# A transformer block with linear attention: attention outputs and down projections as pairs of 64-row matmuls in two parts

## The chip, the core and the metric

The kernel runs on one core of a Trainium2 chip. Its engines are TensorE (PE, with its weight loads shown as PEld), VectorE (DVE), ScalarE (ACT), GpSimd (POOL) and SyncE (SP), which issues nearly all DMAs. The metric is the device time of one execution in microseconds (us); the median of several runs counts.

## The reference

One layer over 2048 tokens of 448 features, all in bf16. A is linear attention with 16 heads of 28 features, B a gated MLP with 1792 hidden features.

```python
phi = lambda t: jnp.where(t > 0, t + 1, jnp.exp(t)) + 1e-6
def A(x, wqkv, wo):                      # x is the layer-normed input
    q, k, v = split_heads(x @ wqkv)      # 16 heads of 28
    pq, pk = phi(q), phi(k)
    kv = einsum("bhsd,bhse->bhde", pk, v)
    z = einsum("bhsd->bhd", pk)
    o = einsum("bhqd,bhde->bhqe", pq, kv) / (einsum("bhqd,bhd->bhq", pq, z)[..., None] + 1e-6)
    return join_heads(o) @ wo
def B(x, w_gate, w_up, w_down):
    return (gelu_tanh(x @ w_gate) * (x @ w_up)) @ w_down
h = x + A(layernorm(x), wqkv, wo)
out = h + B(layernorm(h), w_gate, w_up, w_down)
```

## The kernel before

The 2048 tokens are 16 tiles of 128. Every operation is a task in a graph (`G.add`); the graph finds what each task waits for by the buffers that it reads and writes. The order of the tasks on each engine is written out by hand as five lists of task numbers (`ORDERS`, lines 15 to 51): PE, ACT, DVE, POOL, SP. Each engine takes its list strictly in order, and waits on counters of the other engines; TensorE never waits for itself.

First stage (to about 39 us). Each tile is layer-normed (L348 and L349 for mean and variance), transposed (by TensorE for the first four tiles, by DMA on SP for the others, L390) and projected to q and k (L404, four matmuls of 128 rows and 448 columns a tile). ScalarE makes exp and relu of q into `eq` and `pq` (L431, L432). phi(k) is multiplied with the normed input into four PSUM banks (L423), and line 462 makes of it the 16 matrices kv. Line 466 masks them to blocks of four heads (`kvm`), and line 471 multiplies each block with its rows of wo: `w2`, four groups of 112 rows. So the attention output is, tile by tile, (pq / den) @ w2.

`a2_pair(p)` handles two tiles, one after the other on VectorE. L483 and L484 finish phi(q); L488 (GpSimd, once VectorE) multiplies it with z; L491, L493 and L494 make 1/den; L495 writes pq/den into `pqn`, with each group of 112 features padded to 128. A DMA transpose on SP (L510; for the first pair TensorE, L504) makes `pqnT` of it. Line 523 is the attention output: for each tile four matmuls of 112 rows and 448 columns that add up in one PSUM bank. L529 adds the residual, then come layer norm and the transpose `hnT` (L558, L560, L561; seven 128-feature slices, so that every 64-feature segment lies in both halves of the partitions).

`gu_chunk` makes gate and up (in chunks of 2, 2, 4, 4 and 4 tiles): line 603 takes rows 0 to 63 for the gate, line 605 rows 64 to 127 for up, as two 64-row matmuls at once, seven pairs for each 128 hidden features. A task gu has 512 columns of gate in one bank and 512 of up in another; two such pairs of banks alternate (`BK_G`, `BK_U`). ScalarE makes the gelu (L623), VectorE the product `hh` (L625), which frees the bank.

`b2_tile(t)` is the down projection of one tile: 14 matmuls of 128 rows and 448 columns (L575), the residual (L579) and the output DMA (L580). The last tile goes in two halves of 224 columns. The down weights `wd_sb` are loaded by one DMA of 1568 KB, which the list of SP has behind the transposes of tiles 2 and 3.

On TensorE's list the work of later tiles stands between that of earlier ones: attention outputs of the pairs 2 to 7 and down projections stand in eight blocks between gate-and-up tasks.

Of the kernel before, what the change touches and what calls it, by code (L numbers as in the profile page):

```python
# [5 lines left out]
BF16 = mybir.dt.bfloat16  # L6
# [44 lines left out]
)  # L51


class _Buf:
    __slots__ = ("name", "writer", "readers")

    def __init__(self, name):
        self.name = name
        self.writer = None
        self.readers = []  # L60

# [5 lines left out]
class _Graph:  # L67
# [7 lines left out]
    def add(self, eng, fn, r=(), w=(), name="", kind="op", after=(), mw=False, cost=()):  # L75
# [6 lines left out]
        def dep(d, k):  # L82
            if d is None or d is t:
                return
            if d.eng == eng == "pe":
                t.after.append(d)
                return
# [83 lines left out]
def bass_sequential_preLN__linear_attn_block__glu_gated_geglu__prompt_kernel(  # L171
# [5 lines left out]
    NK = 7  # L177
# [513 lines left out]
```

## Time and profile before

| | |
|---|---|
| median of 3 runs | 193.96 us (193.29 to 194.66) |
| span of the profiled execution, first to last instruction | 192.2 us (the page gives no other time of it) |
| TensorE busy | 187.5 us, 98%, 1572 matmuls |
| VectorE busy | 131.7 us, 69% |
| ScalarE, GpSimd busy | 78.1 us, 50.6 us |
| gate and up (L603, L605), in the chain that ended last | 34% and 5% (they run side by side) |
| down projections (L575), in that chain | 22% |
| attention outputs (L523), in that chain | 5% |

The chain that ended last is followed back from the last instruction: at each step to what released it, or to the instruction before it on its engine. A row of a group has line, engine, operation, output and inputs, shape and count, then the busy time in us, the mean of one in ns, and the idle time of the engine before it. Durations of matmuls overlap: what one costs is the distance from its start to the next one's. "64*128" is the height of the array in use and its columns, "64x512" rows and columns of the moving operand.

### The profile page before, as it was taken

The numbers are of one execution on the slowest core, as the hardware profiler recorded it, in microseconds if no ns is written. First come the engines' busy times: TensorE is split into PE (matmuls) and PEld (weight loads), VectorE is DVE, ScalarE is ACT, GpSimd is POOL, SyncE is SP. The second block draws the span as 40 slices with busy tenths as digits, with TensorE's granted clock in tenths as the row PEclk, the third lists the DMA queues.
The fourth block names the chain that finished last, engine by engine and source line by source line (L and its number), as shares of the span: only waits on it lengthen the run. The fifth ranks groups of instructions, "written<-read, shape, count | busy, mean of one in ns | idle before, by whom it ended". The sixth has DMA issues, their size and how long they took to land.

```text
span 192.2 us, 4152 instructions
## 1 busy us (share of the span) xinstructions
PE 187.5 (98%) x1572; PEld 108.7 (57%) x1572; DVE 131.7 (69%) x355; ACT 78.1 (41%) x226; POOL 50.6 (26%) x92
## 2 busy tenths in 40 slices
PE   7989999999999999999999999999999999999994
PEld 7544554554778777564444655545556655445454
DVE  2899988999999998979957446736544542244412
ACT  3697836599954243044044420024444420044200
POOL 7068520560263287404190000450000000000000
PEclk9999999999999999999999999999999999999999
DMA  6966558998205866520042124305600001010011
GB/s 192 372 186 82 109 104 172 224 217 122 58 0 112 201 206 124 123 54 1 4 78 46 38 49 95 95 1 124 143 0 3 0 3 46 3 48 3 0 48 48
DMA packets 35331, 16.97 MB, mean 88 GB/s; under 512 B 27696, under 2 KB 34032, under 8 KB 35312
## 3 DMA queue, kind: packets, MB, share of 16 engines
q1 hardware_dynamic: 35168, 16.60, 38.4%
q8 instruction: 12, 0.20, 0.4%
q10 hardware_dynamic: 144, 0.11, 0.2%
q14 instruction: 7, 0.06, 0.1%
HBM read 8.26 MB, written 1.84 MB: 53 GB/s over the span
## 4 chain that ended last, share of the span: by engine, by line
PE 84%; DMA 6%; DVE 4%; ACT 3%; POOL 1%; issue 0%; SPq 0%; DVEq 0%; POOLq 0%
PE ps L603 34%; PE ps L575 22%; PE ps L404 10%; PE ps L423 6%; PE ps L523 5%; PE ps L605 5%; DMA wd_sb<-in_B_w_down_dram 4%; DMA x_sb<-in_A_x_dram 2%; DVE hh L625 1%; DVE st L348 1%; ACT eq L431 1%; ACT pq L432 1%; DVE x_sb L529 1%; PE ps L471 0%; ACT e L415 0%
## 5 line engine op out<-in xcount | busy, mean ns | idle before, releaser
L605 PE MATMUL ps<-hnT,wgu_sb 64*128 64x512 bf16 (+1 forms) x490 | 86.6, 334 | 0.0
L603 PE MATMUL ps<-hnT,wgu_sb 64*128 64x512 bf16 (+1 forms) x490 | 86.4, 333 | 0.1
L623 ACT ACTIVATE gl<-ps 128x256 bf16<-128x256 f32 x112 | 37.1, 380 | 83.7 <-PE ps L605 81.8
L625 DVE TENSOR_TENSOR hh<-ps,gl 128x256 bf16<-128x256 f32 x112 | 42.9, 418 | 30.9 <-ACT gl L623 30.7
L603 PEld LDWEIGHTS ps<-hnT,wgu_sb 64*128 64x128 bf16 x490 | 45.3, 94 | 28.0 <-issue 2.6
L605 PEld LDWEIGHTS ps<-hnT,wgu_sb 64*128 64x128 bf16 x490 | 42.7, 94 | 4.8 <-DVE hh L625 2.0
L575 PE MATMUL ps<-wd_sb,hh 128*128 128x448 bf16 (+1 forms) x238 | 43.6, 342 | 0.1
L575 PEld LDWEIGHTS ps<-wd_sb,hh 128*128 128x128 bf16 x238 | 23.0, 98 | 20.1 <-issue 0.8
L404 PE MATMUL ps<-wqk_sb,xnT 128*128 128x448 bf16 x128 | 27.6, 352 | 0.5 <-ACT xnT L383 0.5
L488 POOL TENSOR_TENSOR t<-pq,zbc 128x448 f32<-128x448 bf16 x15 | 16.6, 1117 | 39.0 <-DVE pq L484 22.2
L579 DVE TENSOR_TENSOR x_sb<-ps,x_sb 128x448 bf16<-128x448 f32 (+1 forms) x17 | 10.0, 591 | 18.2 <-PE ps L575 18.2
L348 DVE BATCH_NORM_STATS2 st<-x_sb 128x6 f32<-128x448 bf16 x32 | 19.3, 612 | 3.7 <-DMA x_sb<-in_A_x_dram 3.7
L404 PEld LDWEIGHTS ps<-wqk_sb,xnT 128*128 128x128 bf16 x128 | 12.1, 98 | 11.6 <-ACT xnT L383 0.8
L423 PE MATMUL ps<-pk,xnn 128*128 128x448 bf16 x64 | 14.1, 352 | 0.0
L523 PE MATMUL ps<-w,pqnT 112*128 112x448 bf16 x64 | 13.6, 353 | 0.3 <-DVE mv L349 0.3
L529 DVE TENSOR_TENSOR x_sb<-ps,x_sb 128x448 bf16<-128x448 f32 x16 | 9.7, 613 | 2.7 <-PE ps L523 2.7
L558 POOL TENSOR_SCALAR hn<-x_sb,nm,rs 128x448 bf16<-128x448 bf16 x14 | 10.5, 755 | 0.8 <-POOL rs L361 0.2
L415 ACT ACTIVATE e<-ps 128x448 bf16<-128x448 f32 x16 | 8.5, 540 | 5.3 <-PE ps L404 5.2
L352 POOL TENSOR_SCALAR nm<-mv 128x1 f32<-128x1 f32 (+1 forms) x19 | 4.1, 220 | 25.1 <-DVE mv L349 24.5
L495 DVE TENSOR_TENSOR pqn<-pq,rd 128x448 bf16<-128x448 bf16 x16 | 9.9, 641 | 0.0
L417 DVE SCALAR_TENSOR_TENSOR pk<-ps,e 128x448 bf16<-128x448 f32 x16 | 9.8, 615 | 0.2
L523 PEld LDWEIGHTS ps<-w,pqnT 112*128 112x128 bf16 x64 | 5.6, 97 | 7.2 <-issue 1.3
(65 smaller groups left out, 130.1 us busy)
## 6 DMA issues: line engine op xcount, KB each, us to landing
out_dram<-x_sb SPq DMA_DIRECT2D x15, 112.0 KB, 1.8
wd_sb<-in_B_w_down_dram SPq DMA_DIRECT2D x1, 1568.0 KB, 7.1
x_sb<-in_A_x_dram SPq DMA_DIRECT2D x3, 448.0 KB, 5.7
wgu_sb<-in_B_w_gate_dram SPq DMA_DIRECT2D x1, 896.0 KB, 12.3
wgu_sb<-in_B_w_up_dram SPq DMA_DIRECT2D x1, 896.0 KB, 16.4
wqk_sb<-in_A_wqkv_dram SPq DMA_DIRECT2D x1, 672.0 KB, 5.0
wgu_sb<-in_B_w_gate_dram SPq DMA_DIRECT2D x1, 672.0 KB, 6.1
wgu_sb<-in_B_w_up_dram SPq DMA_DIRECT2D x1, 672.0 KB, 8.6
```

Of the source, the lines that this page charges most:

```text
L348: op("dve", lambda e: e.bn_stats(st[:, t, :], src_ap), [b_src], [b_st[t]], "bnst%s_%d" % (tag, t))
L404: ins = e.matmul(ps[:, bk, 0:D], xnT[:, t, k, :], wqk_sb[:, k, c0:c0 + D], start=(k == 0), stop=(k == 3))
L423: ins = e.matmul(ps[:, BK_PT[c], 0:D], xnn[:, t % XN_R, c * 128:(c + 1) * 128], pk[:, ip, :], start=(t == 0), stop=(t == T - 1))
L488: op(eng, lambda e, t=t, n=n: e.tensor_tensor(t1[:, n, :], pq[:, t, :], zbc[:, :], ALU.mult), [b_pq[t]] + b_z, [b_t1[n]], "t1%s_%d" % (eng ...
L523: ins = e.matmul(ps[:, BK_OUT[n], 0:D], pqnT[0:GW, i2, n, g, :], w2[:, g, :], start=(g == 0), stop=(g == NG - 1))
L529: op("dve", lambda e, t=t, bo=bo: e.tensor_tensor(x_sb[:, t, :], ps[:, bo, 0:D], x_sb[:, t, :], ALU.add), [b_ps[bo], b_x[t]], [b_x[t]], "h ...
L558: op("pool", lambda e, t=t, sh=sh: e.tensor_scalar(hn[:, sh, 0:D], x_sb[:, t, :], nm2[:, t:t + 1], rs2[:, t:t + 1], ALU.add, ALU.mult), [b ...
L575: ins = e.matmul(psO, hh[:, j, (t % HR) * 128:(t % HR + 1) * 128], wd_sb[:, j, c0:c1], start=(j == 0), stop=(j == NJ - 1))
L603: e.matmul(psG[:, jj * N:(jj + 1) * N], wgu_sb[A_, k, j * 128:(j + 1) * 128], hnT[A_, ka_, c0:c0 + N], start=(k == 0), stop=(k == NK - 1))
L605: ins = e.matmul(psU[:, jj * N:(jj + 1) * N], wgu_sb[B_, k, j * 128:(j + 1) * 128], hnT[B_, kb_, c0:c0 + N], start=(k == 0), stop=(k == NK ...
L623: G.add("act", lambda e, gi=gi, cs_=cs_, psG=psG: e.activation(gl[:, gi, cs_], psG[:, cs_], AF.Gelu_apprx_tanh), r=[b_ps[BK_G[i]]], w=[b_g ...
L625: op("dve", lambda e, dst=dst, srcU=srcU, srcL=srcL: e.tensor_tensor(dst, srcU, srcL, ALU.mult), [b_ps[BK_U[i]], b_glh], [b_ar[j_][t % HR] ...
```

## The change

1. Attention output, pairs 1 to 7. `pqn` holds the 448 features of two tiles one after the other without padding, so that the transpose gives seven slices of 128 for both tiles. Each tile's seven 64-feature segments lie alternately in the lower and the upper half of the partitions, the second tile's the other way round. A pair of 64-row matmuls takes one segment of each tile at once, into the two tiles' banks. Part A has four such pairs, part B (the halves exchanged) three. The first pair of tiles keeps four full-height matmuls a tile.
2. `w2` is made in four slices of 128 rows instead of four of 112 (7 matmuls instead of 4, from `kvz`, which lies in `hh` and is zeroed by GpSimd early; a small VectorE copy makes its last slice). Two DMAs of 168 KB make `w2s`, the same slices with the halves exchanged, in the space of `pt_sb`.
3. Down projection, tiles 0 to 13. `b2_pair` takes two tiles: part A multiplies rows 0 to 63 of one tile beside rows 64 to 127 of the other, for all 14 groups of hidden features, part B the halves exchanged, into the same two banks. The last two tiles keep the old form.
4. Part B waits until part A has ended (`sync`): TensorE waits on its own counter.
5. VectorE's attention steps of the pairs 2 to 7 take both tiles in one instruction, and ScalarE's L493 too; GpSimd's product with z stays tile by tile.
6. The five lists are new. On TensorE's, with gu2 and gu4 the gate-and-up tasks:

```
... q_13 q_15 q_12 q_14 trh_0 trh_1 outA_1 outB_1 gu2_0 gu2_1 outA_2 gu2_2 gu2_3 outB_2
gu2_4 gu2_5 outA_3 gu2_6 outB_3 downA_0 gu2_7 downB_0 gu2_8 ... gu2_11 outA_4 gu2_12 outB_4
gu2_13 downA_1 gu4_14 gu4_15 outA_5 gu4_16 outB_5 gu4_17 downB_1 outA_6 gu4_18 ... gu4_22
outB_6 gu4_23 ... gu4_27 downA_2 gu4_28 outA_7 gu4_29 outB_7 gu4_30 ... gu4_33 downB_2
gu4_34 downA_3 gu4_35 ... gu4_40 downB_3 gu4_41 ... gu4_45 downA_4 gu4_46 ... gu4_49 downB_4
gu4_51 gu4_50 downA_5 gu4_53 gu4_52 downB_5 gu4_55 gu4_54 downA_6 down224_15 downB_6
down448_14 down224_15
```

On SP's: `oT_1 dws0 dws1 oT_2 dwd oT_3 hT_2 hT_3 oT_4 ...` (oT: transposes of `pqn`, dws: the copies of `w2`, dwd: the down weights, hT: transposes of `hn`); before, `oT_1 oT_2 oT_3 hT_2 hT_3 dwd oT_4 ...`. On GpSimd's, `ones mones eps mhalf wqkpad ones2 kvzpad ptpad ident ...`; before, `eps ones wqkpad ident wvpad ones2 ...`.

The core of the diff:

```diff
-    def add(self, eng, fn, r=(), w=(), name="", kind="op", after=(), mw=False, cost=()):
+    def add(self, eng, fn, r=(), w=(), name="", kind="op", after=(), mw=False, cost=(), sync=()):
...
+        self.dep(t, sync)
...
-        kvm = sb("kvm", [GW, NG, GW], BF16)
-        w2 = sb("w2", [GW, NG, D], BF16)
+        w2 = sb("w2", [128, 4, D], BF16)
...
-        pqn = sb("pqn", [128, 2, 2, NG, 128], BF16)
-        pqnT = sb("pqnT", [128, 2, 2, NG, 128], BF16)
+        pqn = sb("pqn", [128, 2, 1024], BF16)
+        pqnT = sb("pqnT", [128, 2, 8, 128], BF16)
...
+        kvz = hh[0:GW, 6:9, :].rearrange("p a b -> p (a b)")
+        w2s = pt_sb[:, 0:3, :]
...
+        op("pool", lambda e: e.memset(kvz[:, GW:15 * GW], 0.0), [], [b_kvm], "kvzpad")
...
+        for c in range(4):
+            def fw2(e, c=c):
+                gs = (c, c + 1) if c < 3 else (3,)
+                ins = None
+                for g in gs:
+                    ins = e.matmul(ps[:, BK_W2[c], 0:D], kvc(g, c), wo_sb[:, g, :], start=(g == gs[0]), stop=(g == gs[-1]))
+                return ins
...
+        for h, (to, of) in enumerate(((A_, B_), (B_, A_))):
+            dma("sp", w2s[to, :, :], w2[of, 0:3, :], [b_w2s[h]], "dws%d" % h, r=b_w2[0:3], after=xts[-1:])
...
+                i, b2 = 2 * (p % 2), slice(a, a + 2)
+                op("dve", lambda e: e.tensor_scalar(eq[:, b2, :], eq[:, b2, :], 1.0, EPS, ALU.min, ALU.add), b_eq[b2], b_eq[b2], "cqP_%d" % p)
+                op("dve", lambda e: e.tensor_tensor(pq[:, b2, :], pq[:, b2, :], eq[:, b2, :], ALU.add), b_eq[b2] + b_pq[b2], b_pq[b2], "aqP_%d" % p)
...
+                op("dve", lambda e: e.tensor_tensor(
+                    pqn[:, i2, 0:2 * D].rearrange("p (h d) -> p h d", d=DH), pq[:, b2, :].rearrange("p n (h d) -> p (n h) d", d=DH),
+                    rd[:, i:i + 2, :].rearrange("p n h -> p (n h)").unsqueeze(2).to_broadcast([128, 2 * H, DH]), ALU.mult),
+                   b_pq[b2] + b_rd[i:i + 2], b_pqn[i2], "pnP_%d" % p)
...
-                            ins = e.matmul(ps[:, BK_OUT[n], 0:D], pqnT[0:GW, i2, n, g, :], w2[:, g, :], start=(g == 0), stop=(g == NG - 1))
...
+                for part, segs in (("A", (0, 2, 4, 6)), ("B", (1, 3, 5))):
+                    def foutp(e, segs=segs):
+                        ins = None
+                        for sg in segs:
+                            ra, rb = (A_, B_) if sg % 2 == 0 else (B_, A_)
+                            e.matmul(ps[:, BK_OUT[0], 0:D], pqnT[ra, i2, sg // 2, :], w2[ra, sg // 2, :], start=(sg == 0), stop=(sg == 5))
+                            ins = e.matmul(ps[:, BK_OUT[1], 0:D], pqnT[rb, i2, 3 + (sg + 1) // 2, :], (w2 if sg == 6 else w2s)[rb, sg // 2, :], start=(sg == 0), stop=(sg == 5))
+                        return ins
+                    parts.append(G.add("pe", foutp, r=b_pqnT[i2] + b_w2 + b_w2s, w=[b_ps[b_] for b_ in BK_OUT], name="out%s_%d" % (part, p), sync=parts[-1:]))
...
+        def b2_pair(p):
+            a = 2 * p
+            sl = [slice((t % HR) * 128, (t % HR + 1) * 128) for t in (a, a + 1)]
+            parts = []
+            for half in range(2):
+                def fdp(e, W, half=half):
+                    ins = None
+                    for j in range(NJ):
+                        W(j)
+                        for n in range(2):
+                            rows = (A_, B_)[(n + half) % 2]
+                            ins = e.matmul(ps[:, BK_O[n], 0:D], hh[rows, j, sl[n]], wd_sb[rows, j, :], start=(half == 0 and j == 0), stop=(half == 1 and j == NJ - 1))
+                    return ins
+                parts.append(G.add("pe", fdp, r=[(b_ar[j][t % HR], j if j >= NJ - 2 else 0) for j in range(NJ) for t in (a, a + 1)] + [b_wd],
+                                   w=[b_ps[b_] for b_ in BK_O], name="down%s_%d" % ("AB"[half], p), mw=True, sync=parts[-1:]))
```

More of the change, by code (lines that the diff above doesn't have):

```diff
@@ L73, in __init__, with dep @@
         self.order = None
-    def add(self, eng, fn, r=(), w=(), name="", kind="op", after=(), mw=False, cost=()):
+    def dep(self, t, ds):
+        for d in ds:
+            if d not in t.deps:
+                t.deps.append(d)
+                d.ncons += 1
+                t.dep_at[d.idx] = 0
+    def add(self, eng, fn, r=(), w=(), name="", kind="op", after=(), mw=False, cost=(), sync=()):
         t = _Task()
@@ L85, in dep @@
             if d.eng == eng == "pe":
+                if d in t.deps:
+                    return
                 t.after.append(d)
@@ L470, in bass_sequential_preLN__linear_attn_block__glu_gated_geglu__prompt_kernel @@
-        for g in range(NG):
-            G.add("pe", lambda e, g=g: e.matmul(ps[0:GW, BK_W2[g], 0:D], kvm[:, g, :], wo_sb[:, g, :], start=True, stop=True),
-                  r=[b_kvm, b_wo], w=[b_ps[BK_W2[g]]], name="w2_%d" % g)
-            if g % 2 == 0:
-                op("act", lambda e, g=g: e.activation(w2[:, g, :], ps[0:GW, BK_W2[g], 0:D], AF.Identity), [b_ps[BK_W2[g]]], [b_w2[g]], "evwA_%d" % g)
-            else:
-                op("dve", lambda e, g=g: e.tensor_copy(w2[:, g, :], ps[0:GW, BK_W2[g], 0:D]), [b_ps[BK_W2[g]]], [b_w2[g]], "evwD_%d" % g)
+           [b_ps[BK_KV], b_mask, b_kvm], [b_kvm], "kvm")
@@ new lines, in bass_sequential_preLN__linear_attn_block__glu_gated_geglu__prompt_kernel, with kvc @@
+        b_kvd = _Buf("kvd")
+        op("dve", lambda e: e.tensor_copy(kvz[:, 4 * D:4 * D + 64], kvz[:, 4 * D - 64:4 * D]), [b_kvm], [b_kvd], "kvd")
+        def kvc(g, c):
+            o = g * D + c * 128 if c < 3 else 4 * D - 64
+            return kvz[:, o:o + 128]
+        for c in range(4):
[5 more added lines that the diff above has]
+                return ins
+            G.add("pe", fw2, r=[b_kvm, b_wo] + ([b_kvd] if c == 3 else []), w=[b_ps[BK_W2[c]]], name="w2_%d" % c)
+            if c % 2 == 0:
+                op("act", lambda e, c=c: e.activation(w2[:, c, :], ps[:, BK_W2[c], 0:D], AF.Identity), [b_ps[BK_W2[c]]], [b_w2[c]], "evwA_%d" % c)
+            else:
+                op("dve", lambda e, c=c: e.tensor_copy(w2[:, c, :], ps[:, BK_W2[c], 0:D]), [b_ps[BK_W2[c]]], [b_w2[c]], "evwD_%d" % c)
@@ L489, in a2_pair @@
[L489 to L498 removed]
+            pst = D if p else 512
@@ L515, in a2_pair, with fout @@
                 dma("sp", wd_sb[:, :, :], B_w_down.rearrange("(j p) n -> p j n", p=128), [b_wd], "dwd", after=[G.all[-1]])
-            for ns in ((0,), (1,)) if p == 0 else ((0, 1),):
-                def fout(e, W, i2=i2, ns=ns):
-                    ins = None
-                    for m, n in enumerate(ns):
+            if p == 0:
+                for n in range(2):
+                    def fout(e, W, n=n):
+                        ins = None
                         for g in range(NG):
-                            W(4 * m + g)
-                            ins = e.matmul(ps[:, BK_OUT[n], 0:D], pqnT[0:GW, i2, n, g, :], w2[:, g, :], start=(g == 0), stop=(g == NG - 1))
-                    return ins
-                G.add("pe", fout, r=[(b_pqnT[i2][n], 4 * m) for m, n in enumerate(ns)] + [(b_w2[g], g) for g in range(NG)],
-                      w=[(b_ps[BK_OUT[n]], 4 * m) for m, n in enumerate(ns)], name="out%d_%d" % (len(ns), a + ns[0]), mw=True)
+                            W(g)
+                            ins = e.matmul(ps[:, BK_OUT[n], 0:D], pqnT[:, i2, 4 * n + g, :], w2[:, g, :], start=(g == 0), stop=(g == NG - 1))
+                        return ins
+                    G.add("pe", fout, r=[(b_pqnT[i2][n], 0)] + [(b_w2[g], g) for g in range(NG)], w=[(b_ps[BK_OUT[n]], 0)], name="out1_%d" % (a + n), mw=True)
+            else:
+                parts = []
[8 more added lines that the diff above has]
+                    parts.append(G.add("pe", foutp, r=b_pqnT[i2] + b_w2 + b_w2s, w=[b_ps[b_] for b_ in BK_OUT], name="out%s_%d" % (part, p), sync=parts[-1:]))
             for t in (a, a + 1):
@@ L635, in bass_sequential_preLN__linear_attn_block__glu_gated_geglu__prompt_kernel @@
             gu_chunk(t0, nt)
-            for t in range(t0, t0 + nt):
-                b2_tile(t)
+            for t in range(t0, t0 + nt, 2):
+                if t < T - 2:
+                    b2_pair(t // 2)
+                else:
+                    b2_tile(t)
+                    b2_tile(t + 1)
             t0 += nt
```

67 lines of the change are left out of this document (40 added, 27 removed), and 68 rows, old and new, of the table ORDERS.

## The prediction

> **What bounds the kernel now.** I read the page's first lines, then the chain of waits, then the stretches, and last TensorE's own timeline around the places that the change touches.
>
> ```profile
> PE 187.5 (98%) x1572; PEld 108.7 (57%) x1572; DVE 131.7 (69%) x355; ACT 78.1 (41%) x226; POOL 50.6 (26%) x92
> PEclk9999999999999999999999999999999999999999
> PE 84%; DMA 6%; DVE 4%; ACT 3%; POOL 1%; issue 0%; SPq 0%; DVEq 0%; POOLq 0%
> ```
>
> TensorE (PE) works almost without a hole at full clock and carries 84% of the chain. So the question is what its stream costs: how many matmuls, at what distance, and what holes. The stretches say where holes could come from.
>
> ```profile
> 50.00:60.00 10.00, 10.00 (x153) 7.53 (x150) 9.55 (x28) 6.52 (x15) 4.92 (x7) 1.00 0.28 54
> 130.00:140.00 10.00, 10.00 (x96) 5.32 (x94) 5.42 (x18) 4.40 (x14) 0.00 (x0) 1.00 0.58 126
> ```
>
> From 10 to 80 us VectorE (third pair of numbers) is busy 9 to 10 of every 10 us, later about half. A late VectorE step can stop TensorE only in the first part.
>
> The distance of matmuls is read from their starts, since the durations (353 and 377 ns) overlap.
>
> ```profile
> 111.53 0.38 PE L603 MATMUL ps<-hnT,wgu_sb 64*128 64x512 bf16 x1
> 111.59 0.38 PE L605 MATMUL ps<-hnT,wgu_sb 64*128 64x512 bf16 x1
> 111.90 1.69 PE L523 MATMUL ps<-w,pqnT 112*128 112x448 bf16 x8
> 113.42 1.30 PE L575 MATMUL ps<-wd_sb,hh 128*128 128x448 bf16 x6
> ```
> ```profile
> 93.69 1.49 PE L575 MATMUL ps<-wd_sb,hh 128*128 128x448 bf16 x7
> 95.11 0.39 PE L603 MATMUL ps<-hnT,wgu_sb 64*128 64x512 bf16 x1
> 95.11 0.39 PE L605 MATMUL ps<-hnT,wgu_sb 64*128 64x512 bf16 x1
> 95.34 0.38 PE L603 MATMUL ps<-hnT,wgu_sb 64*128 64x512 bf16 x1
> ```
> ```profile
> 88.26 1.62 PE ps L523 x8
> 89.88 5.30 PE ps L575 x28
> 118.89 1.52 PE ps L523 x8
> 120.40 5.30 PE ps L575 x28
> ```
>
> Three things are to be seen. First, 28 full-height matmuls of 448 columns take 5.30 us, 189 ns each, or 0.422 ns a column; the pairs L603/L605 of 64 rows run side by side, both in one slot of 215.5 ns for 512 columns (0.421 a column). Second, after a pair the same eight matmuls of L523 cost 1.62 us, after a full-height matmul 1.52. Third, the last L575 before 95.11 starts at 93.69 + 6 x 0.189 = 94.82, so the first pair comes 0.285 later instead of 0.189. Each change between full height and 64-row pairs costs about 0.095 us, in either direction (308 ns instead of 215 at 111.90, 201 instead of 108 in the two-tile chunks). There are 16 such changes: eight blocks of L523/L575 stand between the gate-and-up pairs.
>
> The other holes behind 11 us are few: 0.18 at 18.54 (a transpose's landing), 0.12 at 39.93, 0.10 at 44.31, 0.42 at 47.77, 0.24 at 65.41, 0.20 at 70.30.
>
> ```profile
> 47.77 1.67 PE L523 MATMUL ps<-w,pqnT 112*128 112x448 bf16 x8 [0.26 <-DVE mv L349]
> PEld ps L575 <- DMA wd_sb<-in_B_w_down_dram: 0.4, 1, 0.4
> wgu_sb<-in_B_w_up_dram SPq DMA_DIRECT2D x1, 896.0 KB, 16.4
> DMA to landing us min/median/max: 3.0/3.1/4.1
> ```
>
> The first is a timeline row, then one of the waits, one of the page's DMA issues, and one of line L510's own view. The hole at 47.77 is really the first transposed load of L510, issued at 43.55 and landing 4.1 later, at 47.6, behind the up weights (issued at 30.4, landed at 46.8). The one at 65.41 is tile 3's transpose (issued at 61.1, landed at 65.3), the one at 70.30 the down weights.
>
> **The change, part by part.** The sum is made against the profiled span, 192.2; the page has no other time of that execution. The median of the runs, 193.96, lies 1.76 above it, which I carry as a constant.
>
> *Attention output.* Seven pairs of tiles need 7 slots each (448 features in seven 64-row segments) instead of 8 (four 112-row groups a tile): -7 x 0.189 = -1.32 us. All of it was on TensorE's path. The W2 products go from 4 matmuls to 7, ahead of the pairs in the same stream: +3 x 0.189 = +0.57.
>
> *Down projections.* 14 tiles go from 14 matmuls each to 28 half-height matmuls for two tiles in each of two parts: 28 slots for two tiles, as before. At the pairs' rate 448 columns take 188.6 ns against 189.3: 196 x 0.7 = -0.13. The width of 448 for a pair is not in the trace; its bounds are the 256 pairs (107.7 ns, 0.421 a column) and the 512 pairs (0.421), so I take no more uncertainty than +-0.2 us there.
>
> *Changes of shape.* Of 16, 4 remain: the transposes ahead of the first out pair, and three around the last two tiles, which stay full-height (a half of tile 15 stands between the parts of the last pair). -12 x 0.095 = -1.14.
>
> *Waits of part B on part A.* Fourteen. Behind each stands all of TensorE's stream. In 13 of them one or more gate-and-up groups (at least 1.5 us) or half a tile (1.3 us) stand between, and A's last matmul ends 0.16 us after its slot (352 - 189), so the count is there long before: 0. Only the first pair has B right behind A: drain 0.16 plus a restart, which after a landing is 0.14 (47.63 to 47.77): +0.30; bounds 0.10 (a shape change) and 0.42 (the longest hole).
>
> *Two copies of W2 with halves exchanged* go on SP's queue behind the first transpose, which waits for VectorE until about 43.5. They hold 336 KB. The last 896 KB of weights needed 4.8 us after those before them (42.0 to 46.8), so 336 KB take about 1.8 us; behind 46.8 and the transpose (0.8) they land at 49.4. TensorE wants them after 8 q projections, 7 W2 slots, the two first outputs and the transposes, counted from 39.05: about 49.3. I take +0.2; bounds 0 (issued by 46.0, they land like an output, 1.8 us later) and 1.8 (they take twice as long). In return the old hole at 47.77 is gone, since both transposes of the next stage now stand ahead of the first pair: -0.42.
>
> *Down weights earlier on SP.* They now stand ahead of the transposes of tiles 2 and 3 instead of behind: issued about 51.3, landed about 58.5 (7.1 us). First down part: 51.1 + 7 x 1.51 + 14 x 0.19 = 64.3. The hole at 70.30 goes: -0.20. What is now behind them is the third output transpose (wanted at 61.5) and tile 2's and 3's: the output transpose was issued at 57.4, and lands at 60.5 even if it has to let the weights pass; the two others are wanted only at about 67, so 65.41's hole goes: -0.24. If these covers fail by 1 us, that is 1 us on the path.
>
> *VectorE on two tiles.* A joined instruction saves one instruction's fixed part. Three single L495 took 1.70 us, so 0.55 each where 448 elements at the slope of the rows take about 0.47; five joins save some 0.4 us a pair, 2.4 in all, none of it on the path after 80 us. A joined step also stands longer (about 1.0 us for L495; bounds 0.64, one single, and 1.28, two) in front of an L625 that frees a bank. In the first two chunks gate-and-up groups come every 1.5 us and VectorE has little slack. The same products cost TensorE some 0.1 us there before, under a heavier load, so +0.1; bounds -0.1 and +1.2.
>
> *GpSimd's list.* The zeroed buffer for the W2 products, 1568 columns, takes about 1.5 us (0.47 for 448) ahead of the identity, which is then ready at about 5.1, before the first transposes (5.35): 0. Two small memsets (0.1 each) now stand ahead of the pad that the second weight load on SP waits for, and the loads of x behind it: +0.1, bounds 0 and 0.2.
>
> *End.* The last pair wants all VectorE products of the last group after 12 slots (2.3 us); four gelus and four products in a row take about 2.5: +0.1, bounds 0 and 0.3. The output's landing stays.
>
> Sum: -1.32 + 0.57 - 0.13 - 1.14 + 0.30 + 0.20 - 0.42 - 0.20 - 0.24 + 0.10 + 0.10 + 0.10 = -2.08. Span 190.1, time 191.9.
>
> **The rivals.**
>
> *All holes close.* The 0.18, 0.12 and 0.10 go as well and none of the added waits shows: -2.08 - 0.80 - 0.40 = -3.3, 190.7. For it: VectorE gets lighter. Against: the order of the first 50 us is new everywhere, and its first holes hang on loads.
>
> *Banks come late.* In the first two chunks VectorE's joined steps and the waits for part B (the output sum of a down pair now waits for B) hold back products; 14 groups times 0.1 us, more than the bounds above in sum: 191.9 + 1.5 = 193.4. For it: 9.55 of 10 us busy there. Against: the 0.1 us that they cost before.
>
> *Slower: each wait for part A empties TensorE.* If a wait on TensorE's own count stops the weight loads ahead of it, whatever stands between, each of the 13 other B parts pays drain and restart, 0.30: +3.9, 195.8. It decides from 2.1/13 = 0.16 a wait. For it: no TensorE wait on TensorE stands in this trace. Against: its waits on VectorE and ScalarE that are long fulfilled cost nothing between the gate-and-up groups.
>
> *Pairs that don't run side by side at 448.* Row: 215.5 ns for both at 512, so two-fold gain. The Trainium skill, TensorE: Matmul & The Clock Gate, section Why this matters for your kernels, gives 3.07 times for four row tiles at once, short of 4. An estimate by that page's shortfall (1.30 a slot) would be 245 x 57 ns = +14 us, 206. The trace has nearly a thousand of these matmuls without it. The rival in rows: pairs at one after the other in a tenth of the slots, 24 x 0.19 = +4.6, 196.5.
>
> **How the numbers follow.** Forecast 0.57, all holes close 0.10, banks late 0.16, emptying waits 0.14, pairs apart 0.03. The forecast itself spreads from 190.9 to 193.0 by its bounds. 1% is 1.9 us, about what a measurement of this kernel can tell from no change. Faster by more (under 192.0): two thirds of the forecast and the first rival, 0.48. Slower by more (over 195.9): half of the emptying waits, pairs apart and a little for what I don't see, 0.12. Within: 0.40. The range from 190.4 to 195.0 leaves out a few in a hundred below, and the upper parts of the last two rivals.
>
> **What would show it.** Right: eight out slots become seven in the groups of the pair lines; starts of the first down pair follow a gate-and-up pair by 0.11 to 0.22 us with no 0.095 extra; TensorE's instructions rise by about 250 at the same busy share; part B starts at the usual distance behind the group ahead of it. Wrong: holes of 0.2 to 0.4 us in front of every B part; a TensorE wait for the W2 copies or for L625's successor in the first 80 us over 0.5 us in sum; a pair's slot over 0.195 us.

## The result, and the profile after

The changed kernel takes 195.62 us (median of 5 runs, 195.39 to 196.23); the kernel before took 194.1 us beside it. The ratio is 1.0078, with a 95% interval from 1.0050 to 1.0105: 0.8% slower, where 191.9 us had been forecast, and 0.6 us above the forecast's range. The profiled span grew from 192.2 to 193.9 us; the forecast said 190.1. So 3.8 us of span are to be explained.

The page of after, in the lines that answer to those shown of before:

```profile
span 193.9 us, 4577 instructions
...
PE 187.6 (97%) x1813; PEld 109.6 (57%) x1813; DVE 131.4 (68%) x326; ACT 77.0 (40%) x220; POOL 52.3 (27%) x93
...
PEclk9999999999999999999999999999999999999999
...
PE 83%; DVE 10%; ACT 3%; issue 2%; DMA 1%; ACTq 0%; DVEq 0%
```

TensorE has 241 more instructions, the clock is full as before, and VectorE is busy no longer than before. What differs is the chain that ended last: VectorE's share went from 4% to 10%. That says which engine is waited for, not where. The stretches (from and to, length, then busy time and instructions of PE, PEld, DVE, ACT and POOL) say where:

```profile
30.00:40.00 10.00, 9.48 (x63) 5.06 (x61) 8.51 (x16) 6.44 (x15) 3.63 (x4) 1.00 1.06 219
40.00:50.00 10.00, 9.01 (x53) 4.52 (x52) 9.93 (x24) 7.97 (x21) 2.35 (x2) 1.00 0.76 160
50.00:60.00 10.00, 9.94 (x156) 7.62 (x155) 9.66 (x23) 7.46 (x17) 4.01 (x5) 1.00 0.64 185
...
130.00:140.00 10.00, 9.89 (x96) 5.39 (x94) 6.24 (x18) 2.54 (x9) 5.26 (x10) 1.00 0.04 12
```

TensorE is idle for 1.5 us between 30 and 50 us, and a little later on. In its own timeline the holes stand by name:

```profile
38.88 1.03 PE L473 MATMUL ps<-pt_sb,wv_sb 128*112 128x112 bf16 x16 [0.52 <-DVE pt_sb L467]
...
41.53 1.50 PE L493 MATMUL ps<-wo_sb,hh 112*128 112x448 bf16 x7
43.91 0.40 PE L545 MATMUL ps<-ident,pqn 128*128 128x128 bf16 x4 [0.88 <-DVE w L499]
```

Measured by the distances of starts, as in the prediction, TensorE loses 0.68 us ahead of kv (L473), 0.28 within the W2 products (L493), 1.05 ahead of the first transpose of `pqn` (L545), 0.57 in the second down pair (86.4 us), and 0.25 to 0.30 ahead of each of five gate-and-up groups (109.5, 112.8, 126.1, 137.9, 153.1). Holes behind 20 us, changes of shape not counted, sum to about 5.3 us, against 1.3 before. TensorE's last slot ends 1.69 us later than before (191.28 against 189.59), so the other terms did save some 2.3 us.

The work of the change itself went as forecast. The first output pair, part A (four slots) and part B (three), and the gate-and-up pair behind them, again in TensorE's timeline:

```profile
51.88 0.35 PE L573 MATMUL ps<-w,pqnT 64*128 64x448 bf16 x1
...
52.30 0.36 PE L573 MATMUL ps<-w,pqnT 64*128 64x448 bf16 x1
...
52.69 0.35 PE L573 MATMUL ps<-w,pqnT 64*128 64x448 bf16 x1
...
52.88 0.27 PE L674 MATMUL ps<-hnT,wgu_sb 64*128 64x256 bf16 x1
```

Part B comes 0.42 us behind A's last matmul instead of 0.19: 0.23 for the drain. The gate pair at 52.88 follows after a plain 0.19: no extra for a change of shape.

### The profile page after: what moved, and what is told of

The parts are those of the page before. It is cut to its first block, busy times and chain, and to the rows that moved or that the text cites. A ratio compares the mean times of both kernels' runs of the same rounds, so it can differ in the third digit from the quotient of the medians.

```text
span 193.9 us, 4577 instructions
## 1 busy us (share of the span) xinstructions
PE 187.6 (97%) x1813; PEld 109.6 (57%) x1813; DVE 131.4 (68%) x326; ACT 77.0 (40%) x220; POOL 52.3 (27%) x93
## 4 chain that ended last, share of the span: by engine, by line
PE 83%; DVE 10%; ACT 3%; issue 2%; DMA 1%; ACTq 0%; DVEq 0%
PE ps L674 29%; PE ps L642 18%; PE ps L672 12%; PE ps L415 9%; PE ps L434 5%; PE ps L624 3%; PE ps L573 3%; DVE hh L694 2%; PE ps L574 2%; ACT gl L692 1%; DMA x_sb<-in_A_x_dram 1%; DVE den L518 1%; DVE pqn L522 1%; DVE st L359 1%; DVE eq L528 1%
## 5 line engine op out<-in xcount | busy, mean ns | idle before, releaser
L674 PE MATMUL ps<-hnT,wgu_sb 64*128 64x512 bf16 (+1 forms) x490 | 89.8, 334 | 0.4
L672 PE MATMUL ps<-hnT,wgu_sb 64*128 64x512 bf16 (+1 forms) x490 | 89.8, 333 | 0.0
L674 PEld LDWEIGHTS ps<-hnT,wgu_sb 64*128 64x128 bf16 x490 | 44.4, 94 | 31.0 <-DVE hh L694 6.9
L672 PEld LDWEIGHTS ps<-hnT,wgu_sb 64*128 64x128 bf16 x490 | 44.8, 94 | 6.5 <-DVE hnT L606 0.2
L642 PE MATMUL ps<-wd_sb,hh 64*128 64x448 bf16 x392 | 41.7, 349 | 0.2 <-DVE hh L694 0.2
L642 PEld LDWEIGHTS ps<-wd_sb,hh 64*128 64x128 bf16 x392 | 23.4, 94 | 14.9 <-DVE hh L694 1.6
L531 POOL TENSOR_TENSOR t<-pq,zbc 128x448 f32<-128x448 bf16 x12 | 12.6, 1067 | 16.5 <-DVE pq L529 16.5
L648 DVE TENSOR_TENSOR x_sb<-ps,x_sb 128x448 bf16<-128x448 f32 x14 | 8.4, 618 | 7.7 <-PE ps L642 7.7
L573 PE MATMUL ps<-w,pqnT 64*128 64x448 bf16 x49 | 11.5, 349 | 0.1
L399 POOL TENSOR_SCALAR xnn<-x_sb,nm,rs 128x448 bf16<-128x448 bf16 x12 | 9.6, 804 | 3.5 <-ACT rs L368 3.1
L608 POOL TENSOR_SCALAR hn<-x_sb,nm,rs 128x448 bf16<-128x448 bf16 x14 | 10.3, 745 | 0.5
L574 PE MATMUL ps<-pt_sb,pqnT 64*128 64x448 bf16 x42 | 10.2, 350 | 0.0
L371 POOL TENSOR_SCALAR ln<-mv 128x2 f32<-128x2 f32 x7 | 1.5, 222 | 32.1 <-DVE mv L360 31.9
L579 DVE TENSOR_TENSOR x_sb<-ps,x_sb 128x448 bf16<-128x448 f32 x16 | 9.7, 615 | 0.7 <-PE ps L574 0.6
```

The source lines that it names most:

```text
L531: op("pool", lambda e, n=n: e.tensor_tensor(t1[:, n, :], pq[:, a + n, :], zbc[:, :], ALU.mult), [b_pq[a + n]] + b_z, [b_t1[n]], "t1p_%d" % ...
L573: e.matmul(ps[:, BK_OUT[0], 0:D], pqnT[ra, i2, sg // 2, :], w2[ra, sg // 2, :], start=(sg == 0), stop=(sg == 5))
L574: ins = e.matmul(ps[:, BK_OUT[1], 0:D], pqnT[rb, i2, 3 + (sg + 1) // 2, :], (w2 if sg == 6 else w2s)[rb, sg // 2, :], start=(sg == 0), sto ...
L608: op("pool", lambda e, t=t, sh=sh: e.tensor_scalar(hn[:, sh, 0:D], x_sb[:, t, :], nm2[:, t:t + 1], rs2[:, t:t + 1], ALU.add, ALU.mult), [b ...
L642: ins = e.matmul(ps[:, BK_O[n], 0:D], hh[rows, j, sl[n]], wd_sb[rows, j, :], start=(half == 0 and j == 0), stop=(half == 1 and j == NJ - 1))
L672: e.matmul(psG[:, jj * N:(jj + 1) * N], wgu_sb[A_, k, j * 128:(j + 1) * 128], hnT[A_, ka_, c0:c0 + N], start=(k == 0), stop=(k == NK - 1))
```

## The first cause: GpSimd holds VectorE's steps

What made VectorE late at 38.8 and 43.9? Its own timeline in after, and GpSimd's beside it (start, duration; a row may hold several instructions):

```profile
36.19 0.56 DVE L518 TENSOR_REDUCE den<-t 128x16 f32<-128x448 f32 x1
36.66 1.63 DVE L528 TENSOR_SCALAR eq<-eq 128x896 bf16<-128x896 bf16 x1
38.21 0.61 DVE L467 CAST pt_sb<-ps 128x448 bf16<-128x448 f32 x1
...
40.33 0.61 DVE L522 TENSOR_TENSOR pqn<-pq,rd 128x448 bf16<-128x448 bf16 x1
40.87 0.61 DVE L477 TENSOR_TENSOR hh<-ps,mask 112x448 bf16<-112x448 f32 x1
...
41.96 1.36 DVE L522 TENSOR_TENSOR pqn<-pq,rd 128x448 bf16<-128x448 bf16 x1
43.24 0.61 DVE L499 CAST w<-ps 128x448 bf16<-128x448 f32 x1
...
83.76 1.75 DVE L536 TENSOR_TENSOR pqn<-pq,rd 128x896 bf16<-128x896 bf16 x1
```
```profile
36.00 2.04 POOL L515 TENSOR_TENSOR t<-pq,zbc 128x448 f32<-128x448 bf16 x2
40.49 2.35 POOL L531 TENSOR_TENSOR t<-pq,zbc 128x448 f32<-128x448 bf16 x2 [2.44 <-DVE pq L529]
...
82.53 2.04 POOL L531 TENSOR_TENSOR t<-pq,zbc 128x448 f32<-128x448 bf16 x2 [4.53 <-DVE pq L529]
```

Three VectorE steps are long. L528 of the pair 2 (task `cqP_2`) takes 1.63 us where the other instructions of its form take 0.38; L522 of tile 3 (`pn_3`) 1.36 against 0.61 two rows above; L536 of the pair 5 (`pnP_5`) 1.75 against 1.08. Each begins while GpSimd's product with z runs and ends 0.25, 0.48 and 0.95 us behind the end of the second such product (38.04, 42.84 and 84.57), which is its likes' length less 0.13 each time: as if it had begun only there. Behind `cqP_2` stands the eviction L467 that kv wants; behind `pn_3` the copy L499 of `w2`, whose bank the transposes L545 want; behind `pnP_5` the two products of a gate-and-up group that the down pair wants. In the same windows L477 (which reads PSUM) and L518 at 36.19 keep their length. The L522 row at 40.33 began ahead of GpSimd's product and was not held either; GpSimd's row is the longer one then (2.35 for two products, not 2.04).

The Trainium skill, SBUF — State Buffer, section SBUF: two separate sides, states such a rule: GpSimd shares a pair of memory ports with VectorE, and whichever of a GpSimd operation and a VectorE operation "in a 2-port perf mode, or with two SBUF inputs" starts first has them for its whole length. The rows agree, in both directions; whether L528, which has one input, runs in such a mode no row shows. The prediction had not used the rule.

The kernel before has the same products, and its list kept the two apart in the head: three L495 stood at 41.82 with 1.70 us in all, right behind the end of GpSimd's product at 41.61. Later one L495 did fall into a product, took 1.04 us instead of 0.62, and no hole of TensorE followed beyond a change of shape. VectorE's and GpSimd's timelines of before:

```profile
41.82 1.70 DVE L495 TENSOR_TENSOR pqn<-pq,rd 128x448 bf16<-128x448 bf16 x3
...
79.99 1.04 DVE L495 TENSOR_TENSOR pqn<-pq,rd 128x448 bf16<-128x448 bf16 x1
```
```profile
38.26 3.35 POOL L488 TENSOR_TENSOR t<-pq,zbc 128x448 f32<-128x448 bf16 x3 [0.39 <-DVE den L491]
...
79.52 2.43 POOL L488 TENSOR_TENSOR t<-pq,zbc 128x448 f32<-128x448 bf16 x2 [2.90 <-DVE pq L484]
```

So the sign stood in the trace on which the prediction was made.

**Experiment e1: the first held step moved.** In VectorE's list only, `cqP_2` goes behind the eviction and two reductions, right ahead of `aqP_2` (L529), which stood there already:

```diff
-dr_1 cqP_2 evpD_2 dr_2 dr_3 aqP_2 pn_0
+dr_1 evpD_2 dr_2 dr_3 cqP_2 aqP_2 pn_0
```

> Only VectorE's list is changed: cqP_2 and aqP_2, the joined steps of the tiles 4 and 5, go behind evpD_2, dr_2 and dr_3. In the changed kernel cqP_2 took 1.63 us (its likes: 0.38) and ended 0.25 us after GpSimd's second product with z, so evpD_2 came late, kv started 0.68 us late, and w2_1 0.28. Theory one, GpSimd's product keeps VectorE's step out of SBUF until it ends: behind the two products cqP_2 takes about 0.4 us, the holes of 0.68 and 0.28 in front of kv and w2_1 fall to under 0.2 in sum, and the time falls by 0.5 to 0.9 us, since GpSimd's next two products now meet pn_0 to pn_3 in the same way. Theory two, the joined form itself is slow when its inputs have just come from ScalarE: it takes 1.6 us again in the new place, and kv is late by less but the sum of the holes in front of kv, w2_1 and tro_0 (2.0 us) stays within 0.3.

194.70 us, ratio to before 1.0024 [1.0007, 1.0042]; against after's 195.62 it is 0.9 us less. VectorE's timeline of it:

```profile
38.29 0.38 DVE L528 TENSOR_SCALAR eq<-eq 128x896 bf16<-128x896 bf16 x1
...
40.89 1.36 DVE L522 TENSOR_TENSOR pqn<-pq,rd 128x448 bf16<-128x448 bf16 x1
```

The same step behind GpSimd's end takes 0.38; the hole ahead of kv is gone, and 0.24 of the 0.28 within the W2 products stays. `pn_3`, which still falls into the next product (to 41.77), is as long as before, and the hole ahead of L545 stays at 1.05.

**Experiment e9: GpSimd's product taken away, lists untouched.** This is the test that leaves the order alone.

```diff
-e.tensor_tensor(t1[:, n, :], pq[:, a + n, :], zbc[:, :], ALU.mult)
+e.memset(t1[:, n, :], 1.0)
```

> The changed kernel with all its lists as they are; only GpSimd's product with z (t1p) is a memset of the same 448 columns instead, so the denominators of the attention are left out and GpSimd reads nothing. It takes about 0.5 us instead of 1.04. Theory (GpSimd's product reads the memory that VectorE's step reads and holds that step until it is over): cqP_2, pn_3 and pnP_5 stand in the same places of VectorE's list and take 0.38, 0.61 and 1.08 us as their likes do, instead of 1.63, 1.36 and 1.76; the holes ahead of kv (0.68), tro_0 (1.05) and downA_1 (0.57) go or shrink to under 0.3, the time falls by 1.3 to 2.2 us: 193.4 to 194.3. Rival 1 (any work of GpSimd holds it, whether it reads or only writes): each of the three still ends just behind the end of a memset, and takes up to 0.5 us more than its likes. Rival 2 (the steps are long by what they read or by their place): 1.63, 1.36 and 1.76 as before, time 195.6.

192.83 us, 0.9940 [0.9921, 0.9959]; span 191.4 against 193.9. VectorE's timeline and GpSimd's:

```profile
36.65 0.38 DVE L528 TENSOR_SCALAR eq<-eq 128x896 bf16<-128x896 bf16 x1
36.94 0.62 DVE L467 CAST pt_sb<-ps 128x448 bf16<-128x448 f32 x1
...
40.50 0.56 DVE L522 TENSOR_TENSOR pqn<-pq,rd 128x448 bf16<-128x448 bf16 x1
...
81.75 1.09 DVE L536 TENSOR_TENSOR pqn<-pq,rd 128x896 bf16<-128x896 bf16 x1
```
```profile
35.68 0.47 POOL L515 MEMSET t<- 128x448 f32 x1 [0.62 <-DVE den L518]
36.79 0.64 POOL L515 MEMSET t<- 128x448 f32 x1 [0.63 <-DVE den L518]
39.20 0.89 POOL L531 MEMSET t<- 128x448 f32 x2 [1.77 <-DVE pq L529]
```

All three steps are short in the same places of the list, so rival 2 falls. Rival 1 is not put to the test: none of the three starts within a memset here (those near them run from 35.68 to 36.15, 36.79 to 37.43, 39.20 to 40.09 and 80.49 to 81.37). The four holes, 0.68 + 0.28 + 1.05 + 0.57 = 2.58 us, are gone, and the span is 2.5 us shorter, somewhat more than expected. The memset at 36.79 began while L528 ran and took 0.64 instead of 0.47. A memset is also shorter than the product and reads nothing, so this run does not tell whether reading or length counts; it tells that the three steps are long only where GpSimd's product runs beside them.

**Experiment e3: the head's order made anew.** VectorE's list from `dr_1` to the first gate-and-up products was written so that the steps TensorE waits for come first and the steps of two memory inputs lie outside GpSimd's products (`pn_0` and `kvm` ahead, `cqP_2` and `aqP_2` behind `pn_2`, `drP_2` to `pnP_2` behind the layer norms of tiles 0 and 1). One step of ScalarE's list moves with them.

> Only lists are changed, ahead of the first gate-and-up group: on VectorE's, all steps with two SBUF inputs stand outside GpSimd's products with z (pn_0 to pn_3 ahead of cqP_2 and aqP_2, which release the products of the tiles 4 and 5; drP_2 behind the second tile's norm; rdP_2 and pnP_2 behind evhD_1; drP_3 behind the products of group 0), and on ScalarE's deP_2 goes behind rq_15. If GpSimd's products are what made VectorE late, pn_3 falls from 1.36 to 0.62 us, the holes in front of kv, w2_1 and tro_0 (0.68, 0.28, 1.05) fall under 0.4 in sum, and the time falls by 1.2 to 1.8 us against the changed kernel. If the head is late because VectorE simply has too much to do there, the holes move to the transposes and the first gate-and-up group, and the time falls by under 0.8.

194.67 us, 1.0035 [1.0018, 1.0053]: 0.95 less than after, under what was expected. The three holes of the head are gone and the first output pair starts 2.2 us earlier (49.13 instead of 51.30). But `pnP_2` still ends at 51.65 (51.71 in after), its transpose lands at 54.64, and the second output pair waits 1.02 us for it. Half of the gain turned into a new wait.

**Experiment e8: only `pnP_5` moved**, behind both products of the group 13.

```diff
-rdP_5 pnP_5 hr_8 hm0_13 hm1_13 drP_6
+rdP_5 hr_8 hm0_13 hm1_13 pnP_5 drP_6
```

> Only VectorE's list is changed: pnP_5 goes behind both products of group 13. In the changed kernel it took 1.76 us (its likes: 1.09) from 83.76, while GpSimd made the products with z of the tiles 12 and 13 until 84.57, and the second down part waited 0.43 and 0.14 us for the two products behind it. By the theory of the held SBUF port it takes about 1.1 us in the new place, where GpSimd is idle, the hole of 0.57 us in that down part vanishes and the time falls by 0.4 to 0.6 us. If the step is long by its own, it stays at 1.7 us there, and the hole vanishes all the same, since the products now stand ahead; the duration tells the two apart.

195.43 us, 1.0075 [1.0049, 1.0101]: not to be told from after's 195.62, where 0.4 to 0.6 less was expected. The step is short now, and the hole in the down pair is gone, but the step ends at 86.64 instead of 85.51, and the output pair behind it waits 0.94 us for its transpose (landed at 90.28). The wait has moved.

**Experiment e6: joined steps single again** for the pairs 2 to 7, the lists expanded in place.

```diff
-            if p < 2:
+            if p < P:
```

> VectorE's and ScalarE's attention steps of the pairs 2 to 7 are single again, each joined step replaced in place by the two singles (15 of the forecast's terms: five joins a pair). By the forecast's term, VectorE's busy time rises by 0.4 us a pair, 2.4 in all, and TensorE's holes in the first 90 us grow: +0.2 to +0.8 us. If joined steps were what holds banks back or what meets GpSimd's lock more badly, the time falls instead, by 0.3 us or more; cqP_2's 1.63 us would then be two steps, of which only the first is held.

196.24 us, 1.0120 [1.0095, 1.0146]: 0.6 more than after. So joining itself helps here, by 0.6 us, and it saves VectorE 1.9 us of busy time (133.3 in e6, 131.4 in after), near the 2.4 of the prediction. Single steps are held likewise: 1.50, 1.46 and 1.40 us for three of them. Not the width of the steps but their place beside GpSimd's products costs time.

## The second cause: two lists in crossed order

The five holes of 0.25 to 0.30 us stand in the last 90 us, where VectorE is busy half the time. ScalarE makes the gelu of a group in two halves, VectorE the product of each half. In 20 of 56 groups the new lists have the halves in opposite orders on the two engines; in the kernel before in 6. ScalarE, VectorE and TensorE at the group that ends at 107.9 in after:

```profile
107.97 0.71 ACT L692 ACTIVATE gl<-ps 128x256 bf16<-128x256 f32 x2 [1.42 <-PE ps L674]
```
```profile
107.51 0.86 DVE L610 COPY hn<-hn 128x448 bf16<-128x448 bf16 x2
108.71 0.76 DVE L694 TENSOR_TENSOR hh<-ps,gl 128x256 bf16<-128x256 f32 x2 [0.34 <-ACT gl L692]
```
```profile
109.01 0.38 PE L674 MATMUL ps<-hnT,wgu_sb 64*128 64x512 bf16 x1
...
109.52 0.39 PE L674 MATMUL ps<-hnT,wgu_sb 64*128 64x512 bf16 x1
```

VectorE's first product wants the gelu that ends last (108.67), so it idles 0.34 us with the other gelu ready at 108.35. The bank is free at 109.46, 1.59 us behind the group's end at 107.87. The group after the next, which takes the same banks, has its second pair ready some 1.3 us behind that end, but starts it at 109.52, 0.51 us behind the first instead of 0.215: the hole is 0.30.

**Experiment e2: products in the gelus' order.** In 20 groups the two products change places in VectorE's list, nothing else; one of them:

```diff
-hm0_23 hm1_23
+hm1_23 hm0_23
```

> Only VectorE's list is changed: in the 20 gate-and-up groups in which VectorE takes the two products in the other order than ScalarE makes the two gelus, they change places. Theory one, the crossed order keeps the bank 0.3 us longer (product of the second gelu first, 1.59 us from the group's end to the bank's release, against 1.30 where the orders agree) and in the four-tile chunks, where the next use of the bank comes 1.3 us after that end, each crossed group that has no other work in between shows as a hole: the holes of 0.25 to 0.30 us at 109.52, 112.82, 126.14, 137.94 and 153.11 vanish, the time falls by 1.2 to 1.5 us. Theory two, the banks are late because part B of the down pairs or the joined steps hold VectorE back: these holes stay within 0.1 us each, and the time changes by under 0.4 us.

194.36 us, 1.0007 [0.9990, 1.0025]: 1.26 less than after. VectorE and TensorE at the same group:

```profile
107.25 0.84 DVE L610 COPY hn<-hn 128x448 bf16<-128x448 bf16 x2
108.13 0.76 DVE L694 TENSOR_TENSOR hh<-ps,gl 128x256 bf16<-128x256 f32 x2
```
```profile
108.96 0.38 PE L674 MATMUL ps<-hnT,wgu_sb 64*128 64x512 bf16 x1
...
109.18 0.38 PE L674 MATMUL ps<-hnT,wgu_sb 64*128 64x512 bf16 x1
```

The product starts right behind the first gelu, the bank is free 1.27 us behind the group's end (108.88 against 107.61), and the next pair follows at the plain distance. All five holes are gone; one of 0.12 grew to 0.43, as a group now waits for the transposed load of tile 9.

**Experiment e11: both causes taken away at once**, the memset of e9 with the list of e2.

> The memset in place of GpSimd's product with z (the denominators of the attention are left out) together with the twenty products in the order of the gelus; nothing else differs from the changed kernel. Theory (the two causes make up the whole of what the forecast missed and don't depend on each other): span 191.4 - 1.3 = 190.1 and time about 191.6, within 0.5 of the forecast's 190.1 and 191.9; the holes of 0.25 to 0.30 us behind 100 us are gone, those in the head too, and 0.23 ahead of the first part B stays. Rival (they share a part, a group that is released earlier only waits for the next thing, as the transposed load of tile 9 did): span 190.7 or more, with a hole of 0.4 or more at gu4_28.

191.81 us, 0.9894 [0.9871, 0.9917]; span 190.1. That is the forecast, 191.9 and 190.1, with these two causes taken out: 193.9 - 190.1 = 3.8 us, of which e9 alone took 2.5 and e2 alone 1.4 (span 192.5). They add up, and the wait for tile 9 is only 0.24. It is no kernel to use, since it leaves the denominators out.

A single span is less exact than these sums look: TensorE's work ahead of kv, which none of these edits is meant to change, ends anywhere between 37.7 and 38.7 us from profile to profile. Counted from that end to the end of TensorE's last slot, after takes 153.08 us, e9 2.58 less, e2 1.10 less and e11 3.95 less; the kernel before takes 1.72 less.

## The forecast's own disputes, tried

**Experiment e4: down projections full-height, in the same places.** Part A becomes the 14 full-height matmuls of one tile, part B those of the other, so shapes change again around each part.

```diff
-for n in range(2):
-    rows = (A_, B_)[(n + half) % 2]
-    ins = e.matmul(ps[:, BK_O[n], 0:D], hh[rows, j, sl[n]], wd_sb[rows, j, :], ...
+ins = e.matmul(ps[:, BK_O[half], 0:D], hh[:, j, sl[half]], wd_sb[:, j, :], ...
```

> The down projections of the tiles 0 to 13 are full-height again, in the same places of the same lists with the same waits: part A is the first tile's 14 matmuls, part B the second's. Slots and columns stay the same, 28 for two tiles. If a change between full height and pairs costs 0.095 us in either direction, 27 such changes come back and 3 at the end go: +2.3 us on TensorE's stream, of which up to a third may fall into holes that wait for banks: +1.5 to +2.3. If the gain of the pairs was not in these changes, or the pairs of 448 columns cost more than a full-height matmul, the time stays within 0.5 us or falls.

197.98 us, 1.0193 [1.0162, 1.0224]: 2.4 more than after, a little above the expected range. In TensorE's timeline (L640 is the down projection there):

```profile
128.81 0.38 PE L672 MATMUL ps<-hnT,wgu_sb 64*128 64x512 bf16 x1
129.11 2.82 PE L640 MATMUL ps<-wd_sb,hh 128*128 128x448 bf16 x14
131.87 0.39 PE L670 MATMUL ps<-hnT,wgu_sb 64*128 64x512 bf16 x1
```

Into the part 0.30 us instead of 0.215, out of it 131.87 - 129.11 - 13 x 0.189 = 0.30 instead of 0.189: some 0.09 to 0.11 a change. Twelve parts between gate-and-up groups have two changes each, the last block one at its start and three fewer inside: 22 changes net, 2.1 us. Counted from the end of TensorE's work ahead of kv, e4 takes 2.0 us more than after; the rest of its 2.4 arose before that. So the saving of shape changes was real and rightly sized.

**Experiment e5: every part B right behind its part A.** TensorE's list alone is changed, and every wait of B on A becomes a drain.

```diff
-downA_1 gu4_14 gu4_15 outA_5 gu4_16 outB_5 gu4_17 downB_1
+downA_1 downB_1 gu4_14 gu4_15 outA_5 outB_5 gu4_16 gu4_17
```

> Only TensorE's list is changed: every part B stands right behind its part A, as in the changed kernel only the first output pair does (0.23 us from the end of A's stream to B's start). Theory one, the wait of TensorE for its own count costs the drain and restart only when nothing stands in between: 12 more holes of 0.23 us, +2.8 us, less up to 1 us where a hole in front of a gate-and-up group takes it up: +1.8 to +2.8. Theory two, the wait costs the same wherever B stands (the slower rival of the forecast): no more than 0.5 us either way. The output sums of the down pairs come earlier here.

211.3 us, 1.0880 [1.0849, 1.0912]: 15.7 more than after, far beyond every expectation. The drains themselves came out as sized, 0.22 to 0.24 us each. The rest are waits of another kind; one of each is in this timeline of TensorE:

```profile
100.49 0.35 PE L574 MATMUL ps<-w,pqnT 64*128 64x448 bf16 x1
...
100.92 0.36 PE L574 MATMUL ps<-pt_sb,pqnT 64*128 64x448 bf16 x1
...
101.49 0.38 PE L672 MATMUL ps<-hnT,wgu_sb 64*128 64x512 bf16 x1
103.11 0.39 PE L674 MATMUL ps<-hnT,wgu_sb 64*128 64x512 bf16 x1 [1.24 <-DVE hh L694]
```

At 100.92 part B stands 0.43 behind A's last slot (the drain, 0.23 over the slot). At 103.11 TensorE waits for a bank for 1.4 us beyond the slot: ScalarE's and VectorE's lists still have their steps in the order for which the parts were apart. That the lists are the reason is argued from their order and was not tried by itself. What the run does settle: a drain costs about 0.23 where B stands right behind A, and in after no part B that stands apart from its A shows it.

**Experiments e7 and e10: a version that beats both.** e7 takes e3's order of the head, the gelus' order of e2, `pnP_5` as in e8, and moves some layer-norm steps behind the products that TensorE waits for (`drP_5`, `wrap_6`, `cqP_7` and `bnst2_8`, `fo448_2` with four aggregates, `wrap_15` and `wrap_12`). Only lists differ from after.

> Lists alone: the new head, pnP_5 behind group 13's products, all products in their gelus' order, and a few VectorE steps moved behind the product that TensorE waits for next (drP_5, wrap_6, cqP_7, bnst2_8, wraps of 12 and 15, and the norm of the tiles 8 to 11 earlier). If the change's own saving is there (7 fewer slots less 3, 12 fewer changes of shape: 1.9 us) and all that hid it is the holes of the lists, the sum of the holes behind 20 us falls from 5.4 to under 2 us and the time lies at 190.5 to 192.0, under the kernel before. If the slower stream is the pairs' own doing (waits for part B, 64-row matmuls of 448 columns), the time stays over 193.5.

192.50 us (192.18 to 193.1), 0.9931 [0.9905, 0.9957]: 0.7% faster than before, and 0.5 us above the slower end of what was expected. The three largest holes that are left all wait for a transposed load: 0.93 (second output pair), 0.41 (fifth) and 0.46 (tile 9). Others remain, one of 0.29 in front of a down pair and 0.23 ahead of the first part B among them. e10 tries the first of them by one move:

```diff
-drP_2 cqP_4 cqP_3 evhD_1 rdP_2 pnP_2 aqP_3
+drP_2 evhD_1 rdP_2 pnP_2 cqP_4 cqP_3 aqP_3
```

> The best lists so far with one move: VectorE's cqP_4 and cqP_3 stand behind pnP_2 instead of ahead of evhD_1. Theory (the hole of 0.93 us ahead of outA_2 is the lateness of pnP_2, which its transpose carries on): pnP_2 ends 0.5 to 0.8 us earlier (50.5 to 50.8 instead of 51.27), the transpose lands as much earlier, the hole falls to 0.2 to 0.5, the time to 191.8 to 192.2. Rival (the wait moves on again: aqP_3 and drP_3, which follow, come late for outA_3, or evhD_1 finds trh_1 late): 192.4 to 192.8, with a new hole of 0.4 or more at outA_3 or gu2_0.

192.98 us, 0.9945 [0.9917, 0.9972], not to be told from e7. `pnP_2` ends at 51.11, only 0.16 earlier, as `drP_2` itself came later. The hole fell to 0.59, and a new one of 0.82 stands at the gate-and-up group 3. The rival was right in kind, though the new hole is not at the places that it named: in this stretch VectorE has little free time (9.76 of 10 us busy from 50 to 60 us in e7), and a step that is moved ahead makes another late.

## Why the prediction was wrong, point by point

- *Attention output* (-1.32), *W2* (+0.57): as forecast. *Pair width* (-0.13): nearly nothing, since 14 pair slots of a down part take 2.648 us, 0.1891 each against 0.1893 for full height. The rival of pairs that don't run side by side falls, and with it the estimate after the 3.07 times of the Trainium skill (TensorE: Matmul & The Clock Gate, section Why this matters for your kernels).
- *Changes of shape* (-1.14): four are left, 0.09 to 0.10 each; e4 brings most of the others back for 2.0 to 2.4 us.
- *First part B* (+0.30): 0.23 measured. The other 13 cost nothing, as forecast, and the slower rival (each wait empties TensorE wherever it stands) falls.
- *W2 copies* (+0.20): 0. They landed at 50.32 and were wanted at 51.2, as TensorE was late; in e9, without that lateness, they landed at 48.55 and were wanted at 49.2.
- *Holes that go* (-0.42, -0.20, -0.24): they went.
- *VectorE on two tiles* (+0.10, bounds -0.1 and +1.2): **this step failed**, by 3.8 us. It asked how long the joined steps are and looked at the two gate-and-up chunks. It took a step's duration from a row in which GpSimd was at rest, and never laid VectorE's new list beside GpSimd's; and it rested on "A late VectorE step can stop TensorE only in the first part", while five holes of 0.25 to 0.30 us stand behind 109 us, where VectorE is about half idle. The first half cost 2.5 us (e9), the second 1.3 (e2). In their place the prediction had +0.10.
- *The rest of the sum*: e11 shows that it was right together, but not term by term, so that its agreement to 0.1 us is in part luck. The W2 copies and the end (0.30 in sum) show no hole, the small term for GpSimd's list can't be told from the scatter ahead of kv, and the old holes of 0.18 at 18.54 and 0.12 at 39.93 closed, which the sum had left standing; against that e11 has the wait for tile 9 (0.24), which the sum had not, and holes of 0.10 to 0.13 at three gate-and-up groups. The kernel before was not run with the memset; in its trace no hole of TensorE follows the one step that a product with z held.
- *Rivals*: "banks come late" had the right engine, but its place, the first two chunks, shows 0.22 us at one group and the 0.57 of the second down pair, not 0.1 at each of 14 groups. Of the signs named beforehand, "a TensorE wait for L625's successor" did stand up in the waits view, but not in the first 80 us alone, and the wait for the transposes' bank had not been named.

The waits view of after has both causes in three lines (total, times, longest), to be set against 2.0 us for the product's line before:

```profile
PEld ps L674 <- DVE hh L694: 6.9, 18, 0.6
...
PEld ps L545 <- DVE w L499: 1.3, 1, 1.3
...
PEld ps L473 <- DVE pt_sb L467: 1.0, 1, 1.0
```

## What to carry to other kernels

A new hand-made order changes which instructions run at the same time on VectorE and GpSimd: lay both lists side by side, and count a VectorE step of a kind that was held here (tensor_scalar, tensor_tensor or copy of bf16 between SBUF buffers) at its length plus what is left of GpSimd's operation, unless it starts first. Where two engines hand halves of a tile to each other, the order of the halves must be the same on both; an engine that is half idle can still be 0.3 us late, again and again. And when a wait is taken away on a saturated engine, look for the transfer or step that comes next, since half of the gain may go there.

## What the runs showed of the hardware that had not been expected

- A VectorE step that starts within GpSimd's product can be held over the one that GpSimd starts right behind it as well: L528 waited from 36.66 to 38.04, over two products of 1.04 us each. Others got in at the change of products: L495 of before at 79.99 ended 0.47 us behind the first one's end (80.56), and GpSimd's second took 1.42; the small copy L482 of after at 41.56 took 0.32 instead of the 0.14 of e9. What decides is open.
- GpSimd's layer norms hold VectorE too, not the product with z alone: the copy L610 of after at 77.52 took 0.61 us where its likes take 0.27, beside a GpSimd L608 that ended at 78.00.
- It works the other way too, for a write-only operation: 0.64 us instead of 0.47 for the memset that began within L528.
- TensorE's wait for its own last matmuls costs 0.22 to 0.24 us where nothing stands between, less than the 0.30 built up from a drain and a restart after a landing.
